# A chunked retention kernel with a routed feed-forward: gate weights as one row, three comparisons moved to ScalarE, wider filler products and a new written-out order

## Chip, cores and metric

One Trainium2 core of eight. The metric is the device time of one execution in microseconds (us), the median of three runs. Engines are named as the profile names them: PE (TensorE), PEld (its weight loads), DVE (VectorE), ACT (ScalarE), POOL (GpSimd), SP (the queue from which the ordinary transfers are issued).

## What is computed

```python
# attention: q, k, v of shape (4, 8, 768, 64); head h decays by gamma[h]
state = gamma * state + k_t (outer) v_t           # per token t
y_t   = scale * q_t @ state
x = y as (B, S, 512)
# routed feed-forward, per batch b: the 128 tokens with the highest score
scores = x @ w_gate
top = the 128 best of the 768 tokens
out[top] = x[top] + sigmoid(scores[top]) * (relu(x[top] @ w1) @ w2)     # w1: 512 x 1024, w2: 1024 x 512
out[others] = x[others]
```

## The kernel before

The work is cut into 12 units: 4 batches of 3 units, each 256 tokens of all 8 heads. A unit loads 512 KB each of q, k and v, brings them to bf16 with the decay factors, turns them on PE, copies the results out of PSUM, and computes for its two chunks of 128 tokens the masked scores, the chunk's output and the running state. A batch's third unit is followed by its routing: a rank is counted for each token by comparing its score with all others, the 128 best are picked, run through two products with w1 and w2, and added into the rows of the output that were stored before.

Every piece of work is a named task with an engine, the tasks that it needs, and its buffers. `Plan.run` (line 111) issues the tasks in the sequence of the text `ORDER` (line 21), so that text alone sets the order on every engine: each engine runs its own tasks in that order and waits at the first whose inputs are missing. In an item such as `tk.0:1+3@A`, `@` picks one of the allowed engines, `:` names the PSUM banks, and `+3` puts three filler products (`warm_f`, line 202) before the task, products of a constant with itself whose result is overwritten. Task names used below, u being the unit and c its chunk:

- `lq.u lk.u lv.u` loads, `st.u.c` stores, `lw` the load of the gate weights, `w1.i w2.i` the eight loads of the feed-forward's weights, all on SP. There are five buffers each for q, k and v (`DEPTH`, line 18), shared with the weights, and 14 for finished chunks (`xo`).
- `qc kc vc` casts after the load (lines 361, 415, 417; POOL, some on ACT or DVE), `tq tk tv` turns on PE and `eq ek ev` their copies (371, 384, 392), `bk bv` and `fk fv` the same a second time (404, 405).
- `sc.u.c` the scores (440), `mk` the mask on DVE (442), `yo ys` the output products (464, 466), `up es` the state (478, 480), `ey.u.c` the copy of a chunk's output (483), `ga.u.c` its gate scores on DVE (484).
- `pr.u` the scores spread over a row on PE (509), `cp.u` its copy (530), `cd.u.c` and `co.u.c` the comparisons within the unit and with earlier units (520, 526; line 523 is the instruction), `cnt` the counts (629), `rk oh` rank and picked tokens (639, 646), `ix ic gc` their index and gate (670 to 672), `gat sa` gather and scatter (681, 711), `tn ex hu hr dn ad` the feed-forward, `cw1.i.h cw2.i.h` the casts of its weights (312), `yb` bf16 copies of the last batch's chunks (491).
- `tw ew`: the 512 gate weights on all 128 partitions (lines 289 to 298): four numbers a partition are loaded, four turns on PE spread them, a copy puts them in order into `wgB`, which every `ga` reads.

The last batch's products with w1 and w2 are cut finer and mixed with those of batch 2, whose gather comes late.

Of the kernel before, what the change touches and what calls it, by code (L numbers as in the profile page):

```python
# [21 lines left out]
lq.0 lk.0 cf lq.1 cp4 cp1 cp5 cp7 cp3 cp2 cp6 cd0 cz0 lw ca0 cd1 cd3 cd4 ca3 qc.0.1@D qc.0.0@P tq.0:0+26 eq.0@D ca4  # L22
kc.0.0@P kc.0.1@A lv.0 lk.1 tk.0:1 ek.0@A sc.0.1:10 mk.0.1.0 mk.0.1.1 sc.0.0:23 bk.0:4 qc.1.0 qc.1.1 vc.0.0@D tw:5
tq.1:1 fk.0@A kc.1.0@A lv.1 vc.0.1@P tv.0:4+5 ev.0@A lk.2 kc.1.1@P tk.1:0+1 lq.2 vc.1.1 vc.1.0 lv.2 lk.3 ek.1@A lq.3
bv.0:4 fv.0@A qc.2.0 qc.2.1 lv.3 vc.2.1 vc.2.0 qc.3.0 qc.3.1 mk.0.0.0 mk.0.0.1 eq.1@D ew@D sc.1.0:01 mk.1.0.0
# [41 lines left out]
hu.3.2.1 hu.3.0.1 hu.3.1.1 hu.2.0:2 hr.3.0@D hr.3.1@D hr.3.2@A hr.3.3@D hr.2.0@A hu.2.1:4 dn.2.0:2 sa.1 sa.0 gat.3
dn.3.1.0:0 dn.3.0.0:3 hr.2.1@D dn.2.1 ad.2 sa.2 dn.3.0.1 dn.3.1.1 dn.3.0.2 dn.3.1.2 dn.3.0.3 dn.3.1.3 ad.3.0 ad.3.1
sa.3
"""  # L70
# [682 lines left out]
```

## Time and profile before

| | |
|---|---|
| median of three runs | 98.91 us (98.85, 98.91, 100.12) |
| profiled execution, its own time | 98.33 us |
| its span, first to last instruction | 96.6 us |
| around the span | 1.73 us |
| TensorE clock granted, mean | 0.967 of full |
| moved by DMA | 31.67 MB |

A row of a timeline reads: start, duration, engine, line, operation, output and inputs, shapes, count; in brackets the idle time of the engine before it and what ended it. Rows next to each other can overlap, because an instruction's start does not wait for its forerunner's last element; the step from start to start is then what an engine spends on one.

### The profile page before, as it was taken

The numbers are of one execution on the slowest core, as the hardware profiler recorded it, in microseconds if no ns is written. First come the engines' busy times: TensorE is split into PE (matmuls) and PEld (weight loads), VectorE is DVE, ScalarE is ACT, GpSimd is POOL, SyncE is SP. The second block draws the span as 40 slices with busy tenths as digits, with TensorE's granted clock in tenths as the row PEclk, the third lists the DMA queues.
The fourth block names the chain that finished last, engine by engine and source line by source line (L and its number), as shares of the span: only waits on it lengthen the run. The fifth ranks groups of instructions, "written<-read, shape, count | busy, mean of one in ns | idle before, by whom it ended". The sixth has DMA issues, their size and how long they took to land.

```text
span 96.6 us, 3508 instructions
## 1 busy us (share of the span) xinstructions
PE 85.0 (88%) x1370; PEld 72.6 (75%) x1373; DVE 79.5 (82%) x240; ACT 71.5 (74%) x152; POOL 76.5 (79%) x113
## 2 busy tenths in 40 slices
PE   4717899999999999999999999999999999999800
PEld 4615687989899888887899789987899765997500
DVE  5333699999999999999999999999999996862510
ACT  6422249999999999999999999999999970132000
POOL 6580897999999999998989999999998765480250
PEclk9997599999999999999999999999999999999985
DMA  0899999999999899999999999999999996153031
GB/s 7 287 369 362 392 390 392 384 385 403 389 390 404 280 386 265 357 401 404 400 392 392 399 396 398 408 410 409 404 414 411 396 396 221 75 217 109 0 148 70
DMA packets 15199, 31.67 MB, mean 328 GB/s; under 512 B 1360, under 2 KB 1360, under 8 KB 15184
## 3 DMA queue, kind: packets, MB, share of 16 engines
q1 hardware_dynamic: 14544, 29.37, 81.5%
q0 software_dynamic: 640, 2.10, 5.9%
q8 instruction: 10, 0.16, 0.7%
q14 instruction: 5, 0.04, 0.1%
HBM read 24.12 MB, written 7.34 MB: 326 GB/s over the span
## 4 chain that ended last, share of the span: by engine, by line
DMA 45%; POOL 17%; PE 16%; issue 8%; SPq 7%; POOLq 1%; ACT 1%; DVE 0%
DMA qf<-in_q_dram 26%; DMA wf<-in_moe_w_dram 19%; POOL qb L170 8%; SPq L342 5%; POOL vq L170 4%; PE pd L556 2%; PE py L450 2%; POOL kq L167 2%; PE tv L382 2%; SPq L487 2%; PE pg L573 2%; POOLq L748 1%; PE bv L402 1%; POOL w2s L167 1%; PE tq L368 1%
## 5 line engine op out<-in xcount | busy, mean ns | idle before, releaser
L442 DVE TENSOR_TENSOR A<-ps,causal 128x512 bf16<-128x512 f32 x48 | 31.0, 685 | 1.7 <-PE ps L437 1.4
L170 POOL TENSOR_TENSOR qb<-qf,gq 128x512 bf16<-128x512 f32 x23 | 24.4, 1086 | 5.2 <-DMA qf<-in_q_dram 5.1
L170 POOL TENSOR_TENSOR vq<-vf,gv 128x512 bf16<-128x512 f32 x23 | 24.4, 1080 | 0.4 <-DMA vf<-in_v_dram 0.3
L484 DVE SCALAR_TENSOR_TENSOR junk<-py,wgB 128x512 bf16<-128x512 f32 x24 | 16.0, 685 | 0.4 <-ACT xo L163 0.3
L163 ACT ACTIVATE xo<-py 128x512 f32<-128x512 f32 x23 | 14.8, 661 | 0.0
L163 ACT ACTIVATE kq<-kf 128x512 bf16<-128x512 f32 x16 | 10.9, 686 | 3.5 <-DMA kf<-in_k_dram 3.5
L163 ACT ACTIVATE S<-pst 128x512 bf16<-128x512 f32 x20 | 13.4, 669 | 0.0
L450 PE MATMUL py<-vb,A 128*128 128x64 bf16 x192 | 10.7, 192 | 0.0
L368 PE MATMUL tq<-identf,qb 128*128 128x128 f32 x48 | 7.5, 278 | 3.4 <-POOL qb L170 3.2
L437 PE MATMUL ps<-qT,kT 64*128 64x128 bf16 x192 | 9.4, 226 | 0.7 <-ACT kT L163 0.7
L707 POOL DMA_INDIRECT out_dram<-xr,idx x4 | 4.0, 1004 | 7.1 <-DVE xr L702 6.5
L523 DVE TENSOR_SCALAR_CACHE_REDUCE g<-row,sc 128x256 bf16<-128x256 f32 (+1 forms) x16 | 9.6, 608 | 0.0
L163 ACT ACTIVATE kb<-bk 128x512 f32<-128x512 f32 x12 | 7.9, 661 | 2.2 <-PE bk L402 2.2
L516 DVE SCALAR_TENSOR_TENSOR g<-pr,sc,tri 128x128 bf16<-128x128 f32 (+1 forms) x24 | 9.2, 413 | 0.1
L450 PEld LDWEIGHTS <-A 128*128 128x128 bf16 x192 | 8.7, 97 | 0.8
L163 ACT ACTIVATE kT<-tk 128x512 f32<-128x512 f32 x12 | 8.0, 665 | 1.0 <-PE tk L382 1.0
L163 ACT ACTIVATE vT<-tv 128x512 f32<-128x512 f32 x12 | 7.9, 655 | 0.7 <-PE tv L382 0.7
L368 PEld LDWEIGHTS tq<-identf,qb 128*128 128x128 f32 x48 | 5.1, 141 | 4.3 <-POOL qb L170 3.9
L163 ACT ACTIVATE vb<-bv 128x512 f32<-128x512 f32 x12 | 8.1, 672 | 0.2 <-PE bv L402 0.2
L402 PE MATMUL bk<-identf,kT 128*128 128x128 f32 x48 | 8.0, 292 | 0.0
L437 PEld LDWEIGHTS <-kT 64*128 64x128 bf16 x192 | 5.9, 98 | 2.7 <-ACT kT L163 1.0
L402 PE MATMUL bv<-identf,vT 128*128 128x128 f32 x48 | 7.6, 281 | 0.1
(114 smaller groups left out, 199.6 us busy)
## 6 DMA issues: line engine op xcount, KB each, us to landing
qf<-in_q_dram SPq DMA_DIRECT2D x12, 512.0 KB, 8.5
kf<-in_k_dram SPq DMA_DIRECT2D x12, 512.0 KB, 8.7
vf<-in_v_dram SPq DMA_DIRECT2D x12, 512.0 KB, 9.2
out_dram<-xo SPq DMA_DIRECT2D x24, 256.0 KB, 7.7
wf<-in_moe_w_dram SPq DMA_DIRECT2D x8, 512.0 KB, 9.2
xg<-out_dram,idx POOLq DMA_INDIRECT x4, 5.7
out_dram<-xr,idx POOLq DMA_INDIRECT x4, 2.7
wg<-in_moe_w_gate_dram SPq DMA_DIRECT2D x1, 2.0 KB, 7.3
```

The costliest lines, as they stand in the source:

```text
L163: nc.scalar.activation(dst, src, AF.Copy)
L170: (nc.vector if eng == "DVE" else nc.gpsimd).tensor_mul(dst, a, b)
L342: return f, P.add(f"l{nm}.{u}", "SP", lambda e: nc.sync.dma_start(f[:].rearrange("p (e x) -> p e x", e=2), src), bufs=[f])
L368: nc.tensor.transpose(tq[:, j].rearrange("p g h -> p (g h)"), qb[:, j].rearrange("p e d s -> p (e d s)").bitcast(FT), identf)
L402: nc.tensor.transpose(pt[:, c, w, :], words[:, w, C * c:C * c + C], identf)
L437: nc.tensor.matmul(ps[par][:, hp, :], kT[rr, hp // 2, C * c:C * c + C, hp % 2], qT[rr, hp, C * c:C * c + C], start=True, stop=True, skip_g ...
L442: mk = [P.add(f"mk.{u}.{c}.{par}", "DVE", lambda e, par=par, ps=ps, A=A: nc.vector.tensor_mul(A[par][:], ps[par][:], causal[:, None, :].to ...
L450: nc.tensor.matmul(dst, lhsT, rhs, start=not opened, stop=True, skip_group_check=True)
L484: bt["gate"][J] = P.add(f"ga.{u}.{c}", "DVE", lambda e, J=J, py=py, junk=junk: nc.vector.scalar_tensor_tensor(junk[:], py[:].opt(), 1.0, w ...
L516: nc.vector.scalar_tensor_tensor(bt["g"][:, lo + J0:lo + J + 1, :].rearrange("p i t -> p (i t)"), pr[:, :c + 1, :].rearrange("p i t -> p ( ...
L523: nc.vector.tensor_scalar(bt["g"][:, lo:lo + J0, :].rearrange("p i t -> p (i t)"), bt["row"][:, :J0 * C], bt["sc"][:, J:J + 1], 0.0, OP.is ...
L707: apart(b, "rows", nc.gpsimd.indirect_dma_start(out=rows, out_offset=bass.IndirectOffsetOnAxis(ap=idx[:, 0:1], axis=0), in_=xr[:], in_offs ...
```

## The change

Four edits of code, and a new text `ORDER`.

1. The gate weights are loaded as one row of 512 numbers into partition 0 of `wgB`, and one product with a column of ones (`ones1`, set in `cd4`) spreads them over the 128 partitions; the copy `ew` is then contiguous. Before, there were 128 pieces of 16 bytes and four turns.
2. In the last batch `co.u.c` may run on ACT: a sign of (own score minus row), then a sign of (one minus that), which gives 1 where the row is at least the own score; the second pass adds up. The new order puts `co.10.0`, `co.10.1` (128x256) and `co.11.0` (128x512) there; `co.11.1` stays on DVE.
3. The fillers ahead of `tq`, `bk`, `bv` and `pr` are 256 columns wide where they were 128.
4. `ORDER`: k is loaded first, 24 loads are ahead of the first store, and 40 fillers stand where 37 stood (12 of them behind unit 0's start, where 5 stood).

```diff
+    ones1 = consts.tile([1, 128], FT, name="ones1")
-        wg4, bass.AP(tensor=w_gate.tensor, offset=w_gate.offset, ap=[[HP, 128], [1, HP]])))
+        wgB[0:1], bass.AP(tensor=w_gate.tensor, offset=w_gate.offset, ap=[[Dm, 1], [1, Dm]])))
     def turn_w(e):
-        for x in range(HP):
-            nc.tensor.transpose(pw[:, x, :], wg4[:, x:x + 1].to_broadcast([128, 128]), identf)
+        nc.tensor.matmul(pw[:], ones1, wgB[0:1], start=True, stop=True, skip_group_check=True)
-    t_w = P.add("tw", "PE", turn_w, after=[l_w, k_p5], ...
+    t_w = P.add("tw", "PE", turn_w, after=[l_w, k_d4], ...
-        ... warm=warm_f(lambda: tq[:, 0].rearrange("p g h -> p (g h)"))
+        ... warm=warm_f(lambda: tq[:, 0:2].rearrange("p j g h -> p (j g h)"))
                 def far(e, J=J, lo=lo):
+                    if e == "ACT":
+                        g = bt["g"][:, lo:lo + J0, :].rearrange("p i t -> p (i t)")
+                        nc.scalar.activation(g, bt["row"][:, :J0 * C], AF.Sign, bias=bt["sc"][:, J:J + 1], scale=-1.0)
+                        nc.scalar.activation(g, g, AF.Sign, bias=1.0, scale=-1.0, accum_out=bt["far"][:, J:J + 1])
+                        return
-                fr = P.add(f"co.{u}.{c}", "DVE", far, ...
+                fr = P.add(f"co.{u}.{c}", "DVE ACT" if b == LAST else "DVE", far, ...
 ORDER
-lq.0 lk.0 cf lq.1 cp4 cp1 cp5 cp7 cp3 cp2 cp6 cd0 cz0 lw ca0 cd1 cd3 cd4 ca3 qc.0.1@D qc.0.0@P tq.0:0+26 eq.0@D ca4
+lk.0 lq.0 lw lq.1 lv.0 lk.1 lv.1 lk.2 cf cp4 cp1 cp2 cp3 cp5 cp6 cp7 kc.0.1@P cd0 cd1 cd3 cz0 cd4 ca0 ca3 ca4 qc.0.1@D
...
```

What the new order does is seen in three places. The SP queue before, from the first store on (`st.0.0`; the stores are the rows that write `out_0_dram`; the tenth row is `st.2.1`):

```order
L487 DMA out_0_dram<-xo_473 128x512
L342 DMA qf_636<-in_q_dram 128x2x512
L342 DMA qf_638<-in_q_dram 128x2x512
L342 DMA kf_640<-in_k_dram 128x2x512
L342 DMA qf_642<-in_q_dram 128x2x512
L487 DMA out_0_dram<-xo_550 128x512
L342 DMA vf_645<-in_v_dram 128x2x512
L487 DMA out_0_dram<-xo_458 128x512
L342 DMA kf_648<-in_k_dram 128x2x512
L487 DMA out_0_dram<-xo_770 128x512
L342 DMA vf_876<-in_v_dram 128x2x512
L342 DMA qf_878<-in_q_dram 128x2x512
```

The SP queue now, from `lv.7` on (the first store is `st.1.1`, the last row `st.3.1`):

```order
L342 DMA vf_1097<-in_v_dram 128x2x512
L342 DMA kf_1099<-in_k_dram 128x2x512
L342 DMA qf_1273<-in_q_dram 128x2x512
L487 DMA out_0_dram<-xo_630 128x512
L342 DMA qf_1280<-in_q_dram 128x2x512
L487 DMA out_0_dram<-xo_434 128x512
L342 DMA kf_1283<-in_k_dram 128x2x512
L342 DMA vf_1287<-in_v_dram 128x2x512
L342 DMA kf_1289<-in_k_dram 128x2x512
L487 DMA out_0_dram<-xo_805 128x512
L487 DMA out_0_dram<-xo_444 128x512
L487 DMA out_0_dram<-xo_933 128x512
```

Before, `st.2.1` stood ahead of `lv.6` and of unit 7's loads; now these loads stand ahead of every store, and stores of units 0 to 2 wait longer. At the queue's other end 13 stores stand ahead of the last weight load, where 15 stood; 11 follow it, where 9 followed.

The last rows of ACT ahead of the last batch's feed-forward, before (`w2s` rows are casts of weights, `hT` the feed-forward of batches 0 and 1, `gs` is `ge.3`):

```order
L163 ACTIVATE w2s_201<-wf_1655 128x512
L548 ACTIVATE hT_2159<-ph_2209 128x512
L651 ACTIVATE gs_2257<-sc_1859 128x6
L163 ACTIVATE xgT_2252<-pg_2251 128x256 x2
L163 ACTIVATE xo_2117<-py_2116 128x512
L163 ACTIVATE yb_2320<-xo_2117 128x512
L163 ACTIVATE yb_2322<-xo_2014 128x512
L163 ACTIVATE w2s_201<-wf_1660 128x512
L548 ACTIVATE hT_2271<-ph_2270 128x512
L548 ACTIVATE hT_2271<-ph_2325 128x512
```

And now (`g` rows are the sign passes, two for each comparison; `far` holds their sums):

```order
L163 ACTIVATE xgT_2244<-pg_2243 128x256 x2
L163 ACTIVATE w2s_201<-wf_1804 128x512
L525 ACTIVATE g_2214<-row_2237,sc_2002 128x256
L526 ACTIVATE g_2214,far_2275<-g_2214 128x256
L656 ACTIVATE gs_2344<-sc_2002 128x6
L525 ACTIVATE g_2214<-row_2237,sc_2002 128x256
L526 ACTIVATE g_2214,far_2275<-g_2214 128x256
L553 ACTIVATE hT_2293<-ph_2292 128x512
L525 ACTIVATE g_2214<-row_2237,sc_2002 128x512
L526 ACTIVATE g_2214,far_2275<-g_2214 128x512
L553 ACTIVATE hT_2293<-ph_2310 128x512
L163 ACTIVATE yb_2352<-xo_2159 128x512
```

The six passes stand behind the cast of the last weight load (`cw2.3.0`) and around `hr.1.0`, the first half of batch 1's feed-forward; `ey.11.0` and one `yb` have left.

The last comparisons on DVE up to the rank, before (L516 is `cd`, L523 is `co`):

```order
L516 SCALAR_TENSOR_TENSOR g_2094,racc_2093<-pr_2262,sc_1859,tri2_190 128x128
L516 SCALAR_TENSOR_TENSOR g_2094,racc_2093<-pr_2095,sc_1859,tri2_190 128x256
L523 TENSOR_SCALAR g_2094,far_2298<-row_2104,sc_1859 128x256
L516 SCALAR_TENSOR_TENSOR g_2094,racc_2093<-pr_2262,sc_1859,tri2_190 128x256
L671 CAST idx_2302<-pi_2301 128x1
L523 TENSOR_SCALAR g_2094,far_2298<-row_2104,sc_1859 128x256
L523 TENSOR_SCALAR g_2094,far_2298<-row_2104,sc_1859 128x512 x2
L672 RECIPROCAL gt_2303<-pi_2301 128x1
L636 TENSOR_TENSOR rank_2380<-pk_2358,racc_2093 128x2
```

And now:

```order
L516 SCALAR_TENSOR_TENSOR g_2214,racc_2213<-pr_2285,sc_2002,tri2_190 128x256
L165 COPY row_2237<-pr_2285 128x256
L516 SCALAR_TENSOR_TENSOR g_2214,racc_2213<-pr_2215,sc_2002,tri2_190 128x128
L516 SCALAR_TENSOR_TENSOR g_2214,racc_2213<-pr_2327,sc_2002,tri2_190 128x128
L677 RECIPROCAL gt_2257<-pi_2255 128x1
L516 SCALAR_TENSOR_TENSOR g_2214,racc_2213<-pr_2327,sc_2002,tri2_190 128x256
L528 TENSOR_SCALAR g_2214,far_2275<-row_2237,sc_2002 128x512
L165 COPY xo_2159<-py_2158 128x512
L641 TENSOR_TENSOR rank_2381<-pk_2358,racc_2213 128x2
```

Three comparisons are gone from DVE, the copies `cp.10` and `ey.11.0` have come. On PE the same tasks follow `tn.1` up to the counts of the last batch, but `pr.11`, which `cd.11` waits for, now stands behind `hu.1.1` where it stood ahead of `dn.0.0`.

## Rows read from the trace of the kernel before

**Rows 1.** The profile's page: busy time of each engine with its share of the span, and the rate of DMA in 40 slices of 2.4 us.

```profile
PE 85.0 (88%) x1370; PEld 72.6 (75%) x1373; DVE 79.5 (82%) x240; ACT 71.5 (74%) x152; POOL 76.5 (79%) x113
...
GB/s 7 287 369 362 392 390 392 384 385 403 389 390 404 280 386 265 357 401 404 400 392 392 399 396 398 408 410 409 404 414 411 396 396 221 75 217 109 0 148 70
```

**Rows 2.** Busy time by stretch: start and end, length, busy us of each engine with its count, granted TensorE clock, busy share of the DMA engines, GB/s.

```profile
5.00:12.20 7.20, 4.11 (x36) 3.21 (x36) 3.42 (x5) 1.82 (x3) 4.23 (x5) 0.76 1.03 372
15.78:80.22 64.44, 63.51 (x1127) 55.13 (x1124) 63.59 (x192) 63.17 (x136) 59.99 (x81) 1.00 1.03 387
31.40:38.60 7.20, 7.20 (x129) 5.98 (x128) 7.04 (x23) 7.20 (x17) 7.15 (x10) 1.00 0.95 310
74.50:81.90 7.40, 7.13 (x96) 4.93 (x95) 6.62 (x32) 4.51 (x11) 4.88 (x12) 1.00 0.94 345
81.90:91.40 9.50, 9.40 (x127) 7.93 (x127) 5.47 (x13) 1.75 (x4) 3.35 (x4) 1.00 0.30 107
```

**Rows 3.** Timeline of the SP queue around `st.2.1` (the second row).

```profile
25.56 0.60 SPq L342 DMA_DIRECT2D kf<-in_k_dram  x1
30.94 0.34 SPq L487 DMA_DIRECT2D out_dram<-xo  x1
31.37 0.60 SPq L342 DMA_DIRECT2D vf<-in_v_dram  x1
```

**Rows 4.** Timeline of POOL: two casts that wait for loads in the middle of the run.

```profile
44.78 2.08 POOL L170 TENSOR_TENSOR qb<-qf,gq 128x512 bf16<-128x512 f32 x2 [0.48 <-DMA qf<-in_q_dram]
...
49.76 2.08 POOL L170 TENSOR_TENSOR vq<-vf,gv 128x512 bf16<-128x512 f32 x2 [0.26 <-DMA vf<-in_v_dram]
```

**Rows 5.** The chain of waits that ended last, where it leaves the last weight load: start, us, what.

```profile
67.34 9.45 DMA wf<-in_moe_w_dram
...
76.84 0.61 POOL w2s L167
...
78.28 0.62 POOL w2s L167
...
78.94 0.59 PE pd L556 x2
```

**Rows 6.** Timeline of PE from `tn.1` to the last batch's counts; the last row is a weight load of `dn.0.1`.

```profile
74.55 0.64 PE L691 MATMUL pg<-identf,xg 128*128 128x128 f32 x4
...
78.21 1.32 PE L556 MATMUL pd<-w2s,hT 128*128 128x512 bf16 x4
...
80.59 0.42 PE L624 MATMUL pk<-mones,g 128*128 128x1 bf16 x11
80.87 1.02 PE L556 MATMUL pd<-w2s,hT 128*128 128x512 bf16 x4
...
78.94 0.10 PEld L556 LDWEIGHTS <-hT 128*128 128x128 bf16 x1 [0.42 <-issue]
```

**Rows 7.** Timeline of DVE: the start (`vc.0.0`, `eq.1`, `ew`, the first mask of unit 1), then the last comparisons and the rank.

```profile
11.49 1.22 DVE L170 TENSOR_TENSOR vq<-vf,gv 128x512 bf16<-128x512 f32 x1 [0.75 <-ACT kb L163]
...
13.83 0.68 DVE L165 COPY qT<-tq 128x512 f32<-128x512 f32 x1
14.42 1.14 DVE L165 COPY wgB<-pw 128x512 f32<-128x512 f32 x1
15.78 1.29 DVE L442 TENSOR_TENSOR A<-ps,causal 128x512 bf16<-128x512 f32 x2 [0.22 <-PE ps L437]
...
78.40 0.47 DVE L523 TENSOR_SCALAR_CACHE_REDUCE g<-row,sc 128x256 bf16<-128x256 f32 x1
...
78.80 0.74 DVE L523 TENSOR_SCALAR_CACHE_REDUCE g<-row,sc 128x512 bf16<-128x512 f32 x1
...
79.47 0.74 DVE L523 TENSOR_SCALAR_CACHE_REDUCE g<-row,sc 128x512 bf16<-128x512 f32 x1
...
81.05 0.16 DVE L636 TENSOR_TENSOR rank<-pk,racc 128x2 f32<-128x2 f32 x1 [0.75 <-PE pk L624]
```

**Rows 8.** Timeline of ACT: two copies of 128x512 with one of 128x256 between, and the wait in the tail.

```profile
43.55 0.66 ACT L163 ACTIVATE vb<-bv 128x512 f32<-128x512 f32 x1
44.03 0.45 ACT L163 ACTIVATE row<-pr 128x256 f32<-128x256 f32 x1
44.30 0.68 ACT L163 ACTIVATE xo<-py 128x512 f32<-128x512 f32 x1
...
83.12 0.38 ACT L163 ACTIVATE xgT<-pg 128x256 bf16<-128x256 f32 x1 [4.08 <-PE pg L573]
```

**Rows 9.** Timeline of PE: the fillers ahead of `tv.0`.

```profile
12.71 0.71 PE L203 MATMUL tv<-fill 128*128 128x256 bf16 x5
```

**Rows 10.** The gate weights: their transfer (KB, us from issue to landing), their issue, and their turns on PE; then the first cast of unit 1.

```profile
wg<-in_moe_w_gate_dram SPq DMA_DIRECT2D x1, 2.0 KB, 7.3
...
2.87 0.60 SPq L289 DMA_DIRECT2D wg<-in_moe_w_gate_dram  x1
...
10.61 1.06 PE L295 MATMUL pw<-identf,wg 128*128 128x128 f32 x4
...
10.09 2.07 POOL L170 TENSOR_TENSOR qb<-qf,gq 128x512 bf16<-128x512 f32 x2 [2.71 <-DMA qf<-in_q_dram]
```

**Rows 11.** The end: the second batch's sum on DVE, and the last scatter.

```profile
90.11 0.75 DVE L702 SCALAR_TENSOR_TENSOR xr<-pd,gt,xg 128x512 f32<-128x512 f32 x1 [1.50 <-PE pd L556]
...
92.45 0.97 POOL L707 DMA_INDIRECT out_dram<-xr,idx  x1 [0.30 <-issue]
```

More of the change, by code (lines that the diff above doesn't have):

```diff
@@ L67 @@
[L67 to L69 removed]
+lk.0 lq.0 lw lq.1 lv.0 lk.1 lv.1 lk.2 cf cp4 cp1 cp2 cp3 cp5 cp6 cp7 kc.0.1@P cd0 cd1 cd3 cz0 cd4 ca0 ca3 ca4 qc.0.1@D
+kc.0.0@A tk.0:0+19 ek.0@D qc.0.0@P tq.0:1+7 tw:0 vc.0.1@D vc.0.0@D eq.0@A ew@A sc.0.0:12 sc.0.1:34 bk.0:5 fk.0@A lq.2
+qc.1.0 qc.1.1 kc.1.0@P kc.1.1@A tq.1:0 vc.1.0 vc.1.1 eq.1@A tv.0:5+2 mk.0.1.0 mk.0.0.0 mk.0.1.1 mk.0.0.1 tk.1:6
@@ L70 @@
+dn.1.0:5 gat.2 cnt.3.1 ra.3 gh.3 dn.1.1 rk.3 oh.3.0 tn.3.0.0:3 tn.3.1.0:4 oh.3.3 tn.3.0.1 ix.3:1 tn.3.1.1 ad.1 ad.0
+ic.3 ex.3.1@D ex.3.0@A hu.3.1.0:3 hu.3.2.0:6 hu.3.0.0:5 hu.3.1.1 tn.2:4 st.10.1 st.11.0 st.9.1 hu.3.0.1 hu.3.3.0:0
+hu.3.2.1 hu.3.3.1 st.10.0 sa.1 ex.2.0@A ex.2.1@A hu.2.0:4 hr.3.2@A hr.3.0@A hr.3.3@A hr.2.0@A hu.2.1:5 dn.2.0:4 gc.3
+hr.2.1@A hr.3.1@D dn.3.0.0:5 dn.3.1.0:0 dn.2.1 ad.2 dn.3.0.1 sa.0 gat.3 dn.3.1.1 dn.3.0.2 dn.3.1.2 dn.3.0.3 dn.3.1.3
+sa.2 ad.3.0 ad.3.1 sa.3
 """
@@ L259, in c_dve4 @@
         nc.vector.memset(mones, -1.0)
+        nc.vector.memset(ones1, 1.0)
     def c_act0(e):
@@ L289 @@
     l_w = P.add("lw", "SP", lambda e: nc.sync.dma_start(
-        wg4, bass.AP(tensor=w_gate.tensor, offset=w_gate.offset, ap=[[HP, 128], [1, HP]])))
-    pw = P.buf("px", [128, HP, 128], FT, "pw")
+        wgB[0:1], bass.AP(tensor=w_gate.tensor, offset=w_gate.offset, ap=[[Dm, 1], [1, Dm]])))
+    pw = P.buf("px", [128, Dm], FT, "pw")
     def turn_w(e):
-        for x in range(HP):
-            nc.tensor.transpose(pw[:, x, :], wg4[:, x:x + 1].to_broadcast([128, 128]), identf)
-    t_w = P.add("tw", "PE", turn_w, after=[l_w, k_p5], bufs=[pw], warm=warm_f(lambda: pw[:, 0:2].rearrange("p x q -> p (x q)")))
-    k_wgB = P.add("ew", "ACT DVE", lambda e: copy(e, wgB.rearrange("p (q x) -> p x q", x=HP), pw[:]), after=[t_w], bufs=[pw])
+        nc.tensor.matmul(pw[:], ones1, wgB[0:1], start=True, stop=True, skip_group_check=True)
+    t_w = P.add("tw", "PE", turn_w, after=[l_w, k_d4], bufs=[pw], warm=warm_f(lambda: pw[:, :256]))
+    k_wgB = P.add("ew", "ACT DVE", lambda e: copy(e, wgB, pw[:]), after=[t_w], bufs=[pw])
     w_done = {}
@@ L369, in turn_q @@
                                     qb[:, j].rearrange("p e d s -> p (e d s)").bitcast(FT), identf)
-        t_q = P.add(f"tq.{u}", "PE", turn_q, after=qc + [k_p5], bufs=[qb, tq, qT], warm=warm_f(lambda: tq[:, 0].rearrange("p g h -> p (g h)")))
+        t_q = P.add(f"tq.{u}", "PE", turn_q, after=qc + [k_p5], bufs=[qb, tq, qT], warm=warm_f(lambda: tq[:, 0:2].rearrange("p j g h -> p (j g h)")))
         eq = P.add(f"eq.{u}", "ACT DVE", lambda e: copy(
@@ L402, in go @@
                         nc.tensor.transpose(pt[:, c, w, :], words[:, w, C * c:C * c + C], identf)
-            t_ = P.add(f"b{nm}.{u}", "PE", go, after=[e_, k_p5], bufs=[xT, pt, xb], warm=warm_f(lambda: pt[:, 0, 0, :]))
+            t_ = P.add(f"b{nm}.{u}", "PE", go, after=[e_, k_p5], bufs=[xT, pt, xb], warm=warm_f(lambda: pt[:, 0].rearrange("p w d -> p (w d)")))
             return xb, P.add(f"f{nm}.{u}", "ACT DVE", lambda e: copy(
@@ L522, in far @@
                 def far(e, J=J, lo=lo):
+                    if e == "ACT":
[3 more added lines that the diff above has]
+                        return
                     nc.vector.tensor_scalar(bt["g"][:, lo:lo + J0, :].rearrange("p i t -> p (i t)"), bt["row"][:, :J0 * C],
                                             bt["sc"][:, J:J + 1], 0.0, OP.is_ge, OP.add, accum_out=bt["far"][:, J:J + 1])
-                fr = P.add(f"co.{u}.{c}", "DVE", far, after=bt["cp"] + [bt["gate"][J]], bufs=[bt["row"], bt["sc"], bt["g"], bt["far"]])
+                fr = P.add(f"co.{u}.{c}", "DVE ACT" if b == LAST else "DVE", far, after=bt["cp"] + [bt["gate"][J]], bufs=[bt["row"], bt["sc"], bt["g"], bt["far"]])
                 bt["rk"][J].append(fr)
```

87 lines of the change are left out of this document (41 added, 46 removed).

## The prediction, made before the changed kernel ran

> **What bounds the kernel now.** I read the page first, for the balance of the engines. Then I read busy time by stretch, to see where that balance holds, and the chain of waits backwards from the end. Last came the timelines of the engines on which the chain turns: SP, POOL, PE, DVE and ACT.
>
> The page shows no single bound: PE is busy for 88% of the span, DVE 82%, POOL 79%, ACT 74%, and DMA runs near 400 GB/s in most slices [rows 1]. The stretch view divides this. From 15.78 to 80.22 us DVE is busy 63.59 of 64.44 us, PE 63.51, ACT 63.17, and DMA moves 387 GB/s on average [rows 2]. What can be won lies in the start, in a dip of DMA and in the tail. The start is short of data: up to 12.2 us PE is busy 4.11 of 7.20 us at a granted clock of 0.76 [rows 2], and POOL's first cast of unit 1 waits until 10.09 for its load [rows 10]. The dip runs from 31.4 to 38.6, at 310 GB/s [rows 2]. SP issued `lk.6` at 25.56, and then stood at `st.2.1` until 30.94, with `lv.6` behind it until 31.37 [rows 3]. The price comes later: POOL waits 0.48 us for a q at 44.78 and 0.26 for a v at 49.76 [rows 4].
>
> In the tail three things arrive nearly together. The last weight load lands at 67.34 + 9.45 = 76.79, its casts start at 76.84 and 78.28, and `dn.0.1` goes on at 78.94 [rows 5], 0.42 us late [rows 6]. DVE compares until 79.47 + 0.74 = 80.2, then stands 0.75 us, because PE starts the last counts only at 80.59 [rows 6, 7]. From 81.9 to 91.4 PE is busy 9.40 of 9.50 [rows 2], the last scatter starts at 92.45 [rows 11], and the order there hardly changes. So the end moves about as the rank at 81.05 moves.
>
> **The change part by part.**
>
> *The SP queue.* Filling the dip is worth 7.20 x (387 - 310) / 387 = 1.4 us of transfer [rows 2]. Two stores of 0.26 MB moved behind the last weight load are 0.52 MB / 387 GB/s = 1.35 us. The last weight load could land 2.8 us earlier, at 74.0. What then remains of the tail's wait is `dn.0.1`'s 0.42 us; no more than that, because PE's tasks from `tn.1` at 74.55 to the counts are the same ones. I take 0.42. POOL's waits are 0.74 in sum, bounds 0 (the other engines had work meanwhile) and 0.74; I take half, 0.37. The new stall is `st.3.1`, which stands ahead of `lq.9` and all later loads and needs a copy of unit 3. Up to it 28 loads and 4 stores are issued, 15.7 MB. The first 13 slices moved 11.0 MB by 31.4 us [rows 1], so there is work for DMA until about 43 us, and I count that stall at nothing. If its cover went, it would cost what the dip costs now.
>
> *The start.* The gate weights' 128 pieces go. DMA runs at 372 GB/s until 12.2, against 387 later [rows 2], which prices them at no more than 7.20 x 15 / 387 = 0.28 us. On PE `tw` moves ahead of unit 0's scores. The trace has no such product. The four turns took 1.06 us [rows 10], and I bound it by nothing and twice that. The cover is POOL's cast of q, which ends at 10.09 + 2.07 = 12.16 and before which PE has nothing of unit 1; with the load landing 7.3 us after issue as before [rows 10], and issued 0.65 earlier, at about 9.5, that cover just holds. On DVE `vc.0.1` comes (1.22 beside POOL) while `eq.1` (0.59 from start to start) and `ew` (1.14) leave [rows 7]; its masks slip behind both casts: 11.49 + 2 x 1.2 + 4 x 0.6 = 16.3 against 15.78. So the start lies between 0.28 won and 0.5 lost, and I take 0.
>
> *DVE up to the rank.* Gone after the start: `eq.2` and `ey.0.0`, 0.59 each by `eq.1`'s step [rows 7], two comparisons of 0.40 and one of 0.67 (78.40 to 78.80 to 79.47): 2.65 us. Come: `ek.2`, `ey.1.0`, `ey.11.0`, 0.59 each, and `cp.10`, about 0.3: 2.07. Net 0.58, and with the 0.75 that it stands now DVE could give 1.33 us. But PE brings the counts. By PE's busy row, 63.51 of 64.44 us, PE has no room, and 0 reaches the end. By the weight loads' row, 55.13, it has 9 us of room, and all 1.33 can [rows 2]. I take 0.5, nearer to the first, since the last counts are what DVE waited for. The Trainium skill (Trainium Kernel Development and Optimization, Performance Expectations) calls matmul busy time a bad measure of how full PE is, because matmuls are pipelined, and weight-load busy time a good one; taken alone it would give 1.33 here and a time of about 97.0, the busy row alone 98.3. No row of this trace decides between them.
>
> *ACT.* Six passes: by steps 4 x 0.27 + 2 x 0.48 = 2.04 us, by whole durations, since the second pass reads what the first wrote, 4 x 0.45 + 2 x 0.67 = 3.14 [rows 8]. I take the second. ACT is busy 4.51 of 7.40 us from 74.5 [rows 2], then waits 4.08 [rows 8], so 2.9 us of it fit before the counts; what does not fit is the slower rival below.
>
> *Fillers.* Seven more behind unit 0's start, 0.71 / 5 = 0.14 each [rows 9]: 0 to 1.0 us. The low end is a filler that runs while PE would have stood anyway. PE stands 0.93 us in the middle by its busy row and 9 us by its weight loads [rows 2]; I take 0.2, nearer to the second, since a filler fills what the first row calls busy too. Those that are only wider count within that.
>
> Sum: 0.42 + 0.37 + 0.5 - 0.2 = 1.1 us. From the profiled execution's own 98.33 us (span 96.6 and 1.73 around it) that gives 97.2. The median of the runs shown, 98.91, lies 0.58 above that execution, so I predict 97.8.
>
> **The rivals.**
>
> *All of it arrives.* PE has the room that its weight loads show. Then 0.42 + 0.74 + 1.33 + 0.28 = 2.8 us are won: 96.1. For it speaks that DVE has no gap between 15.78 and 80.22, against it that PE was last at 81.05.
>
> *PE is full and only shuffles.* Earlier loads find it busy; the fillers cost their whole 1.0, against 0.42 + 0.37 won: 99.1. For it: 9.40 of 9.50 us in the tail and 63.51 of 64.44 before it.
>
> *Slower: ACT's queue takes the place of DVE's.* The sign passes stand behind the cast of the last weight load and around `hr.1.0`. If that load lands at 76.79 as before, ACT ends the cast at 77.4, `co.10.0` at 78.3, `ge.3` at about 78.5, `co.10.1` at 79.4, `hr.1.0` at 80.0, `co.11.0` at 81.4, and `hr.1.1` at 82.0. `dn.1.1` needs `hr.1.1`, and now starts at 80.87 [rows 6]: 1.1 us late, 100.0. It decides when the last weight load lands later than 76.79 - 1.1 = 75.7. Against it: two stores less ahead of that load.
>
> **How the numbers follow.** My forecast 0.38 (own range 96.9 to 98.6), all of it 0.27, shuffled 0.17, slower 0.18. Within 2%, about what a measurement of this kernel can tell from no change, is 96.9 to 100.9. Faster: 0.24 of the second case and 0.06 of the first, 0.30. Slower: half of the last, which has room above its 1.1 us if the start's 0.5 is lost too, and a little of the third: 0.11. The rest, 0.59, is the same. The range goes from 95.7, a little below the second case, to 100.2, just above the last.
>
> **What would show it.** Right: no dip of DMA between 31 and 39 us; the last weight load landed by 75; `dn.0.1` without a stop; the rank at 80 instead of 81.05; PE as full from the rank to the last scatter as now. The forecast is wrong on DVE's share if DVE still waits for the counts as long, wrong on the SP queue if DMA falls off while SP stands at `st.3.1`, and wrong on ACT if the counts follow `co.11.0`. If unit 1's first mask comes after 16.3 us, the start has cost what I set at nothing.

## The result, and the profile after

The changed kernel takes 97.41 us (median of six runs, 97.03 to 97.60), the kernel before 98.90 beside it (98.53 to 100.12): a ratio of 0.9845, 95% interval 0.9809 to 0.9881, or 1.5 us less. The profiled execution took 97.38 us with a span of 95.7; the one of before took 98.33 with 96.6. The experiments below came in three groups of four, and the kernel before scattered more beside them (99.6 to 101.7, 99.3 to 102.6 and 97.1 to 101.9 us), so their ratios have wider intervals. Ratios leave disturbed runs out, which in the third group left only 5 of the 35 runs of before; there the kernels of the group are compared with each other.

The changed kernel's busy time by stretch, with the columns of [rows 2] (us, PE, PEld, DVE, ACT, POOL, granted clock, DMA share, GB/s):

```profile
5.00:12.20 7.20, 5.74 (x56) 3.71 (x54) 4.34 (x5) 3.00 (x6) 5.15 (x6) 1.00 1.05 391
31.40:38.60 7.20, 7.00 (x128) 6.47 (x126) 6.95 (x23) 7.20 (x17) 7.20 (x9) 1.00 1.05 393
74.50:81.90 7.40, 6.77 (x104) 5.23 (x103) 6.12 (x24) 4.98 (x14) 3.38 (x9) 1.00 0.61 202
81.90:91.40 9.50, 7.97 (x97) 6.45 (x95) 2.85 (x8) 2.88 (x8) 4.04 (x4) 1.00 0.40 142
```

Against [rows 2], three things moved. The dip of DMA is gone (393 GB/s where 310 stood). DMA falls off earlier at the end (202 where 345 stood): SP has issued the last weight load by 63.0 us, where it was 67.7. And in the start the granted clock is 1.00 where 0.76 stood; PE is busy 1.6 us more, which is no more than its fillers there (0.47 + 0.93 + 0.38). The last is the one I had read past. Before, PE was at the low one of its two clock levels (1.2 of 2.4 GHz) for most of the time from 8 to 12 us; the two halves of it show busy us of PE, granted clock, DMA share, GB/s, and below them stands PE's timeline of that start:

```profile
8.00:10.00 2.00, 1.31 (x19) 0.56 1.03 367
10.00:12.00 2.00, 1.67 (x8) 0.59 1.04 394
```

```profile
1.24 2.96 PE L203 MATMUL tq<-fill 128*128 128x128 bf16 x26 [1.24 <-DVE fill L272]
6.88 0.65 PE L368 MATMUL tq<-identf,qb 128*128 128x128 f32 x4 [2.69 <-POOL qb L170]
8.74 1.03 PE L437 MATMUL ps<-qT,kT 64*128 64x128 bf16 x16 [0.69 <-ACT kT L163]
12.22 0.66 PE L368 MATMUL tq<-identf,qb 128*128 128x128 f32 x4 [0.55 <-POOL qb L170]
```

PE stood 2.69 us behind its fillers; the next turns still took 0.65 us, and the 16 scores that came after them 1.03. In the changed kernel it never stands for a whole microsecond there, and the same 16 scores take 0.62 (third row); unit 1's turns come at 10.82 instead of 12.22 (last row):

```profile
6.26 0.93 PE L203 MATMUL tq<-fill 128*128 128x256 bf16 x7
8.14 0.66 PE L368 MATMUL tq<-identf,qb 128*128 128x128 f32 x4 [0.95 <-POOL qb L170]
9.78 0.62 PE L437 MATMUL ps<-qT,kT 64*128 64x128 bf16 x16
...
10.82 0.60 PE L368 MATMUL tq<-identf,qb 128*128 128x128 f32 x4
```

The loads were earlier as well. POOL goes from q of unit 0 into q of unit 1 without a stop (three casts in one row; by [rows 10] unit 1's first cast waited until 10.09), and DVE is at its casts of v at 9.17, where [rows 7] has 11.49 (there the wait before it ended with a copy on ACT, not with its load):

```profile
6.51 3.61 POOL L170 TENSOR_TENSOR qb<-qf,gq 128x512 bf16<-128x512 f32 x3 [0.82 <-DMA qf<-in_q_dram]
```

```profile
9.17 2.52 DVE L170 TENSOR_TENSOR vq<-vf,gv 128x512 bf16<-128x512 f32 x2 [1.40 <-DMA vf<-in_v_dram]
11.61 3.90 DVE L442 TENSOR_TENSOR A<-ps,causal 128x512 bf16<-128x512 f32 x6
```

Unit 1's first mask is the fifth of the six in the last row, so it starts near 14.2 us, where it stood at 15.78 [rows 7].

Now the tail. PE's rows that answer to [rows 6] are 2.0 us earlier at `tn.1` and 2.1 at the last counts; then two waits appear, one for `oh`, one for the second batch's gather:

```profile
72.52 0.63 PE L696 MATMUL pg<-identf,xg 128*128 128x128 f32 x4
...
78.46 0.42 PE L629 MATMUL pk<-mones,g 128*128 128x1 bf16 x11
...
80.40 1.17 PE L578 MATMUL pg<-oh,yb 128*128 128x128 bf16 x18 [0.58 <-DVE oh L648]
...
83.61 0.63 PE L696 MATMUL pg<-identf,xg 128*128 128x128 f32 x4 [0.51 <-DMA xg<-out_dram,idx]
```

ACT, where the sign passes went: the cast of the last weight load starts at 73.73 (that load landed at 76.79 in [rows 5]), and each pass with a sum brings an instruction of its own that reads it out:

```profile
73.73 0.63 ACT L163 ACTIVATE w2s<-wf 128x512 bf16<-128x512 f32 x1
74.25 0.51 ACT L525 ACTIVATE g<-row,sc 128x256 bf16<-128x256 f32 x1
74.85 0.42 ACT L526 ACTIVATE g<-g 128x256 bf16<-128x256 bf16 x1
75.17 0.19 ACT L526 ACTIVATION_READ_ACCUMULATOR g<-g 128x1 f32 x1
75.27 0.19 ACT L656 ACTIVATE gs<-sc 128x6 f32<-128x6 f32 x1
...
76.78 0.71 ACT L525 ACTIVATE g<-row,sc 128x512 bf16<-128x512 f32 x1
...
78.15 0.58 ACT L553 ACTIVATE hT<-ph 128x512 bf16<-128x512 f32 x1
```

By steps, a comparison of 256 costs 75.27 - 74.25 = 1.02 us and that of 512 costs 78.15 - 76.78 = 1.37; with the second of 256 (75.36 to 76.31) some 3.3 in all. DVE and POOL at the rank, and the end (the rows that answer to [rows 7, 11]):

```profile
78.91 0.16 DVE L641 TENSOR_TENSOR rank<-pk,racc 128x2 f32<-128x2 f32 x1 [0.24 <-PE pk L629]
...
79.59 0.16 DVE L642 TENSOR_TENSOR rank<-pk,far 128x4 f32<-128x4 f32 x1 [0.52 <-POOL far L637]
...
89.17 0.75 DVE L707 SCALAR_TENSOR_TENSOR xr<-pd,gt,xg 128x512 f32<-128x512 f32 x1 [5.60 <-PE pd L561]
```

```profile
78.20 1.12 POOL L682 DMA_INDIRECT xg<-out_dram,idx  x1 [2.45 <-DVE g L528]
79.34 0.23 POOL L637 TENSOR_TENSOR far<-far,racc 128x4 f32<-128x4 f32 x1
...
91.52 0.98 POOL L712 DMA_INDIRECT out_dram<-xr,idx  x1 [0.30 <-issue]
```

The rank's first half is 2.14 us earlier than in [rows 7], its second half waits for `ra.3` (`far`), which POOL issues behind the second batch's gather, and the last scatter is 0.93 us earlier than in [rows 11]. So 2 us were won before the tail, and the tail gave about half back: some 0.6 us at `oh`, which starts 1.5 us earlier than before, and some 0.6 behind it, most of that at `tn.2`.

### The profile page after: what moved, and what is told of

It is laid out like the page before. It is cut to its first block, busy times and chain, and to the rows that moved or that the text cites. A ratio compares the mean times of both kernels' runs of the same rounds, so it can differ in the third digit from the quotient of the medians.

```text
span 95.7 us, 3522 instructions
## 1 busy us (share of the span) xinstructions
PE 85.9 (90%) x1371; PEld 72.6 (76%) x1374; DVE 76.9 (80%) x232; ACT 75.3 (79%) x163; POOL 76.2 (80%) x114
## 4 chain that ended last, share of the span: by engine, by line
PE 58%; ACT 13%; DMA 10%; issue 6%; POOL 4%; DVE 2%; SPq 2%; POOLq 2%
PE py L450 10%; PE ps L437 7%; DMA out_dram<-xo 5%; DMA qf<-in_q_dram 5%; PE tq L368 5%; PE bv L402 5%; PE bk L402 5%; PE pst L475 4%; PE tv L382 4%; PE tk L382 4%; PE ph L547 4%; PE pr L507 3%; ACT qT L163 2%; ACT kq L163 2%; ACT xo L163 2%
## 5 line engine op out<-in xcount | busy, mean ns | idle before, releaser
L170 POOL TENSOR_TENSOR vq<-vf,gv 128x512 bf16<-128x512 f32 x22 | 23.1, 1065 | 0.9 <-DMA vf<-in_v_dram 0.8
L163 ACT ACTIVATE xo<-py 128x512 f32<-128x512 f32 x22 | 13.7, 629 | 0.1
L450 PE MATMUL py<-vb,A 128*128 128x64 bf16 x192 | 11.7, 192 | 0.0
L163 ACT ACTIVATE qT<-tq 128x512 f32<-128x512 f32 x12 | 7.7, 640 | 3.2 <-PE tq L368 3.2
L163 ACT ACTIVATE kq<-kf 128x512 bf16<-128x512 f32 x14 | 8.9, 655 | 1.2 <-DMA kf<-in_k_dram 1.2
L516 DVE SCALAR_TENSOR_TENSOR g<-pr,sc,tri 128x256 bf16<-128x256 f32 (+1 forms) x24 | 9.3, 411 | 0.8 <-PE pr L507 0.5
L528 DVE TENSOR_SCALAR_CACHE_REDUCE g<-row,sc 128x512 bf16<-128x512 f32 (+1 forms) x13 | 7.8, 618 | 0.0
L707 DVE SCALAR_TENSOR_TENSOR xr<-pd,gt,xg 128x512 f32<-128x512 f32 (+1 forms) x5 | 3.0, 638 | 5.9 <-PE pd L561 5.6
L682 POOL DMA_INDIRECT xg<-out_dram,idx x4 | 4.6, 1142 | 4.0 <-DVE g L528 2.5
L382 PE MATMUL tk<-ident,kq 128*128 128x128 bf16 x96 | 7.4, 220 | 0.3 <-POOL kq L167 0.3
```

Source lines behind the costliest of these rows:

```text
L163: nc.scalar.activation(dst, src, AF.Copy)
L170: (nc.vector if eng == "DVE" else nc.gpsimd).tensor_mul(dst, a, b)
L382: nc.tensor.transpose(pt[:, j].rearrange("p g h -> p (g h)"), fb[:, j].rearrange("p e d -> p (e d)"), ident)
L450: nc.tensor.matmul(dst, lhsT, rhs, start=not opened, stop=True, skip_group_check=True)
L516: nc.vector.scalar_tensor_tensor(bt["g"][:, lo + J0:lo + J + 1, :].rearrange("p i t -> p (i t)"), pr[:, :c + 1, :].rearrange("p i t -> p ( ...
L528: nc.vector.tensor_scalar(bt["g"][:, lo:lo + J0, :].rearrange("p i t -> p (i t)"), bt["row"][:, :J0 * C], bt["sc"][:, J:J + 1], 0.0, OP.is ...
```

## Experiments

### The start in the old order: loads or clock

The first thought was that the 128 small pieces had held back the loads. The first edit was made alone in the kernel before (`e1_row`), and the pieces were issued later in it (`e5_late_pieces`):

```diff
 e1_row, kernel before, ORDER as it was
-  128 pieces into wg4, four turns
+  one row into wgB, one product with ones1
 e5_late_pieces, kernel before
-... cz0 lw ca0 ...  lv.0 lk.1 tk.0:1
+... cz0 ca0 ...  lv.0 lk.1 lw tk.0:1
```

> The kernel before with the first edit alone: the gate weights come as one row and one product spreads them; the order is the old one. Theory A (the 128 pieces of 16 bytes held back the transfers around them): POOL's first cast of unit 1 starts near 8.1 us as in the changed kernel, not at 10.09, DVE's casts of v come about 2 us earlier, and 1 to 2 us of it reach the end: 97.0 to 98.0 us. Theory B (the new order of the loads did it): that cast stays at 10.0 to 10.1, and the time stays at 98.9 within 0.4.

> The kernel before with its 128 pieces, but their load issued behind that of unit 1's k and so behind six loads where it stood behind three. Theory A: q of unit 1 lands about 2 us earlier (its cast at 8 to 8.5 us) because nothing is in its way yet, and what is issued behind the pieces comes late instead; the turns of the gate weights come 1 to 2 us later. Time between 98.0 and 99.5 us. Theory B: the cast stays at 10.0 to 10.1 and the time at 98.9 within 0.4.

Measured: `e1_row` 103.76 us, ratio 1.041 (1.029 to 1.053); `e5_late_pieces` 101.60, 1.011 (0.997 to 1.025). `e1_row` is slower than either of its theories allows. The interval of `e5_late_pieces` is too wide to part its two; its q of unit 1 is cast at 10.35, near theory B's 10.0 to 10.1 and not at theory A's 8 to 8.5. In `e1_row` q of unit 1 is cast at 8.08, as theory A said, and yet the kernel is 4% slower. Its PE rows show why: from 6.8 to 19 us everything on PE takes nearly twice its duration:

```profile
6.76 1.11 PE L368 MATMUL tq<-identf,qb 128*128 128x128 f32 x4 [2.58 <-POOL qb L170]
...
9.42 1.03 PE L437 MATMUL ps<-qT,kT 64*128 64x128 bf16 x16 [0.69 <-ACT kT L163]
...
11.43 2.07 PE L295 MATMUL pw<-wgB,ones 1*128 1x512 f32 x2
13.43 1.11 PE L368 MATMUL tq<-identf,qb 128*128 128x128 f32 x4
...
19.22 0.66 PE L402 MATMUL bk<-identf,kT 128*128 128x128 f32 x4
```

```profile
12.00:14.00 2.00, 2.00 (x5) 1.00 1.05 392
```

The granted clock reads 1.00 in that stretch (second fence: busy PE, granted clock, DMA share, GB/s), so here only the durations tell the low level. The Trainium skill (TensorE: Matmul & The Clock Gate, Part 1) names these two levels for PE's clock, which depend on how busy PE has been, and says that the recorded clock events have been seen to be unreliable. The rows agree on the levels and on the record: the same 16 scores take 1.03 or 0.62 us, and here 1.03 at a recorded 1.00. With the low level lasting to 19 us, unit 1's first mask came at 18.96 instead of 15.78 [rows 7]. Of the 4.4 us by which this run's last scatter is late (96.87 against 92.45) 3.1 are there at `tn.1` (77.64 against 74.55); the rest arises behind `tn.2`, in a stretch whose length differs between executions of one kernel (last section). The kernel before came back to the high level by 12.22; why `e1_row` took until 19, and `e5_late_pieces`, with its four turns, until 17, is not settled.

### The start again: the fillers

If the clock decides, the fillers do. Three kernels: the changed one with as little filling as before (`e6_cold`), and the old order with more, once with pieces (`e7_warm`) and once with the row (`e8_row_warm`).

```diff
 e6_cold, changed kernel
-tk.0:0+19 ... tq.0:1+7
+tk.0:0+13 ... tq.0:1
 e7_warm, kernel before; e8_row_warm, e1_row
-tq.0:0+26
+tq.0:0+46
```

> The changed kernel with fewer fillers ahead of unit 0's turns: 13 where 19 stood and none where 7 stood, so that PE falls silent near 4.1 us, as before the change, and not near 7.2. Theory A (PE's clock is the start's main gain): the products of the start run at the low clock again (16 scores 1.03 us where the changed kernel shows 0.62), unit 1's first mask comes 1.3 us later or more, and the time is 98.5 to 101 us. Theory B (the earlier loads are the gain): the start's products take 0.62 and 0.66 us as now, the time stays at 97.4 within 0.5.

> The kernel before with 46 fillers ahead of its first turns where 26 stood, so that PE is busy until about 6.5 us and not 4.2. Nothing else is changed: pieces, old order, old loads. Theory A: the low clock between 8 and 12 us (16 scores in 1.03 us, four turns in 1.06 to 1.12) is gone; unit 1's products still wait for its q at 10.1, so unit 1's first mask moves from 15.8 to 15 at best and 0.3 to 0.9 us are won. Theory B (the clock does not hang on these fillers): rows of the start as before, the time equal to before within 0.4 us.

> The kernel before with the first edit (one row, one product), which by itself ran 4% slower, and with 46 first fillers. Theory A (that run lost by the low clock, which lasted until 19 us in it, though its loads were 2 us early): the start's products run at the high clock, unit 1's first mask comes at 13.5 to 14.5 us instead of 18.96, and the time falls by 1 to 2 us below the kernel before. Theory B (the one-row product or the early loads themselves do harm in the old order): still 2% or more slower than before.

Measured: `e6_cold` 100.98 us, 1.004 (0.998 to 1.010); `e7_warm` 100.01, 0.993 (0.988 to 0.998); `e8_row_warm` 99.21, 0.983 (0.978 to 0.988). Theory A holds each time. Without thirteen fillers, some (4.23 - 2.96) + 0.93 = 2.2 us of products that compute nothing, the changed kernel loses all its gain, although its q of unit 1 is cast at 8.59. PE and DVE of `e6_cold`, the last row being unit 1's first mask, 3 us later than in the changed kernel:

```profile
1.24 2.96 PE L203 MATMUL tk<-fill 128*128 128x256 bf16 x13 [1.24 <-DVE fill L273]
...
11.18 1.04 PE L437 MATMUL ps<-qT,kT 64*128 64x128 bf16 x16
```

```profile
17.26 1.29 DVE L442 TENSOR_TENSOR A<-ps,causal 128x512 bf16<-128x512 f32 x2 [2.46 <-PE ps L437]
```

And PE of `e7_warm`, the kernel before with twenty more fillers: behind the fillers no product takes twice its duration, and unit 1's turns stand at 10.26.

```profile
1.24 5.09 PE L203 MATMUL tq<-fill 128*128 128x128 bf16 x46 [1.24 <-DVE fill L272]
...
8.60 0.62 PE L437 MATMUL ps<-qT,kT 64*128 64x128 bf16 x16 [0.69 <-ACT kT L163]
...
10.26 0.66 PE L368 MATMUL tq<-identf,qb 128*128 128x128 f32 x4
```

The last row goes beyond what was expected: q of unit 1 was there two us sooner than in the profile of before, with all 128 pieces in place.

`e8_row_warm` weighs most. It keeps the old order, the old SP queue and every comparison on DVE, and with the row and twenty more fillers alone its ratio, 0.983, is that of the whole change, 0.9845. Beside `e7_warm`, from which it differs by the first edit only, it is 0.8 us faster in the median (the two intervals just meet), so with the clock held the row seems to be worth something in the old order; the start doesn't show where, since unit 1's first mask stands at 14.43 in `e7_warm` and 14.26 in `e8_row_warm`.

### The pieces in the new order, and the later fillers

```diff
 e2_pieces, changed kernel
-  one row into wgB, one product with ones1
+  128 pieces into wg4, four turns
 e4_nofill, changed kernel
-tv.0:5+2 ... tq.2:0+1 ... pr.1:0+2 ...   (14 fillers in ten places)
+tv.0:5 ... tq.2:0 ... pr.1:0 ...
```

> The changed kernel with its first edit undone: 128 pieces and four turns, the load third in the queue as in the changed kernel. Theory A: the loads behind the two first land about 2 us later again (first cast of unit 1 near 10 us instead of 8.1, first cast of v near 11 instead of 9.2), and 0.7 to 2 us of that reach the end: 98.1 to 99.4 us. Theory B: the landings stay as in the changed kernel and the time at 97.4 within 0.4.

> The changed kernel without its 14 fillers behind the first 26. Theory A (my term: a filler mostly runs while PE would have stood, net 0.2 us for seven more): the time falls by no more than 0.4 us, to 97.0 to 97.4, and the granted clock in the start stays at 1.00. Theory B (PE is full, each filler costs its 0.14 us): 14 of them are 2.0 us, the time falls below 96.4. Theory C (the fillers hold the clock): the granted clock falls below 0.95 somewhere in the first 20 us, and the time rises by 0.5 us or more.

Measured: `e2_pieces` 98.56 us, 0.981 (0.967 to 0.995); `e4_nofill` 97.91, 0.978 (0.969 to 0.987). Neither can be told from the changed kernel's 0.9845. For the pieces the profiles don't decide either. POOL's first cast of unit 1 began at 10.35 in `e5_late_pieces` and at 8.13 in `e7_warm`, both with pieces:

```profile
10.35 2.07 POOL L170 TENSOR_TENSOR qb<-qf,gq 128x512 bf16<-128x512 f32 x2 [2.58 <-DMA qf<-in_q_dram]
```

```profile
8.13 2.08 POOL L170 TENSOR_TENSOR qb<-qf,gq 128x512 bf16<-128x512 f32 x2 [0.99 <-DMA qf<-in_q_dram]
```

In the new order it began at 8.71 with pieces, and with the row between 7.9 and 9.21. So when the first loads land changes by up to 2 us from one execution to the next, and what the first edit is worth in the new order stays open. For the later fillers theory C falls (no stretch at the low level), and theory A and B are not parted by the times; the last scatter of `e4_nofill` starts at 91.85, against 91.52 with the fillers, which speaks for A, in one execution of each.

### The comparisons on ACT

```diff
 e3_co_dve, changed kernel
-co.10.0@A ... co.10.1@A hr.1.0@A co.11.0@A
+co.10.0 ... co.10.1 hr.1.0@A co.11.0
```

> The changed kernel with the three comparisons back on DVE, where they stood before. Theory A (my term: DVE's queue ahead of the counts is worth 0.5 us or more): the last counts start 0.8 to 1.6 us later than 78.46 us, and the time rises by 0.4 to 1.2 us. Theory B (the end hangs on batch 2's gather, which POOL issues at 78.2 to 79.3 and tn.2 waits for): the counts come later but the end moves by less than 0.3 us.

Measured: 101.73 us (99.99 to 101.79) beside 100.97 for the kernel before; no ratio could be formed, so the times decide nothing. Its start was late, so distances inside the tail of its one profiled execution are read. From `tn.1` (74.21) to the rank (82.48) it takes 8.27 us, in the changed kernel 78.91 - 72.52 = 6.39; to `oh` (82.74) 8.53, against 7.27; to the last scatter (95.00) 20.79, against 19.00. PE of this run, in the middle of the counts, then DVE:

```profile
81.05 0.25 PE L629 MATMUL pk<-mones,g 128*128 128x1 bf16 x4 [1.49 <-DVE g L528]
```

```profile
82.74 1.02 DVE L648 TENSOR_TENSOR oh<-pk,rank 128x384 bf16<-128x384 f32 x2
...
86.06 0.42 DVE L165 CAST xgT<-pg 128x256 bf16<-128x256 f32 x1 [0.91 <-PE pg L578]
```

The counts wait for DVE's comparisons: 1.9 us at the rank's first half, of which 1.3 reach `oh` (in the changed kernel the second half waits for `ra.3`). The 1.8 us at the last scatter can't all be put down to the comparisons, because behind `oh` comes the pause of the last row, which also stands in `e6_cold` and `e7_warm` (0.90 us each) at the same copy. In this one execution theory B falls, and theory A's 0.8 to 1.6 us at the counts was too small.

### The tail: `ra.3`, the gather, and the old order once more

Could the half that the tail gave back be had? `ra.3` was put ahead of the gather on POOL (`e9_ra`), then also `tn.2` behind eight more products (`e10_ra_tn`), with the changed kernel (`after_again`) and the old order with the new start (`e8_again`) on the same chip.

```diff
 e9_ra, changed kernel
-dn.1.0:5 gat.2 cnt.3.1 ra.3
+dn.1.0:5 ra.3 gat.2 cnt.3.1
 e10_ra_tn, the same and
-hu.3.1.1 tn.2:4 st.10.1 ... hu.3.0.1 hu.3.3.0:0
+hu.3.1.1 st.10.1 ... hu.3.0.1 hu.3.3.0:0 tn.2:4
```

> The changed kernel once more, as the measure for the three beside it, on the same chip. Every theory: 0.98 to 0.99 of the kernel before; POOL's first sum of unit 1 of the last batch's rank (ra.3) issues behind the second batch's gather and the rank's second half waits about 0.5 us for it; tn.2 waits about 0.5 us for that gather.

> The kernel before with the row load and 46 first fillers, beside the changed kernel. Theory A (the start is the whole gain; the refilled SP queue, the passes on ACT and DVE's relief bring nothing over it): equal to the changed kernel within 0.6 us. Theory B (my terms of the middle and the tail, 0.42 + 0.37 + 0.5 us, come on top of the start): 0.7 to 1.3 us slower than the changed kernel.

> The changed kernel with ra.3 ahead of gat.2 on POOL. Theory A (what the start won is given back at the rank, which waits for ra.3 behind the gather): the rank's second half follows its first without a wait, oh starts near 79.2 us instead of 79.79, and the end comes 0.3 to 0.6 us earlier. Theory B (the end hangs on the second batch's gather, at tn.2): the rank is earlier but tn.2 then waits about 1.1 us where it waited 0.5, and the end stays within 0.2 us.

> As the run before, and tn.2 behind eight more products of the last batch on PE. Theory A and B alike: the wait of tn.2 falls below 0.3 us, oh starts near 79.2, and the end comes 0.6 to 1.1 us earlier than in the changed kernel: about 0.990 of it. Theory C (the end hangs on something later, the third gather or the second batch's own chain of products): no gain over the changed kernel beyond 0.2 us.

Measured: `after_again` 97.04 us, 0.992 (0.982 to 1.002); `e8_again` 97.95, 0.988 (0.978 to 0.998); `e9_ra` 98.02, 1.002 (0.992 to 1.011); `e10_ra_tn` 97.94, 0.997 (0.991 to 1.003). The four share their runs of before; beside each other, the two with `ra.3` moved are 0.9 us slower in the median than the changed kernel. In `e9_ra` `tn.2` waits 1.13 us for the gather (first fence), as theory B said, though the end came later than that theory's 0.2 us. In `e10_ra_tn` the rank's wait is gone and `oh` starts at 79.02, but POOL's gather issues at 79.13, where `after_again` has 78.05, and its last scatter starts at 91.45, against 91.28: the 0.62 us won at `oh` are lost again in small waits on PE, 0.27 for the gather (last fence) and 0.30 for the copies behind it among them. POOL, then DVE, then PE of `e10_ra_tn` follow the row of `e9_ra`:

```profile
84.84 0.63 PE L696 MATMUL pg<-identf,xg 128*128 128x128 f32 x4 [1.13 <-DMA xg<-out_dram,idx]
```

```profile
78.17 0.20 POOL L637 TENSOR_TENSOR far<-far,racc 128x4 f32<-128x4 f32 x1 [2.64 <-ACT g L526]
79.13 1.11 POOL L682 DMA_INDIRECT xg<-out_dram,idx  x1 [0.76 <-issue]
```

```profile
79.02 1.02 DVE L648 TENSOR_TENSOR oh<-pk,rank 128x384 bf16<-128x384 f32 x2
```

```profile
83.55 0.63 PE L696 MATMUL pg<-identf,xg 128*128 128x128 f32 x4 [0.27 <-DMA xg<-out_dram,idx]
```

So theory A of `e9_ra` falls and theory C of `e10_ra_tn` holds: whichever of the two POOL does first, the other is late, and PE meets it at `oh` or at `tn.2`. No version here clearly beats the changed kernel.

`e8_again` asks what the rest of the new order brings, and by the ratios it brings nothing that can be told: 0.988 without it and 0.992 with it, and 0.983 for the same kernel in the group before. Theory A holds; theory B's 0.7 to 1.3 us do not show. Its best runs are level with the changed kernel's too (96.48 against 96.49 us); its median over all runs is 0.9 us higher, because half of its runs lie between 98.0 and 99.70. What sets those apart is not shown; one of them was profiled. In that execution (98.0 us) `tn.1` stands at 73.01, 1.5 us before that of [rows 6], and the last counts at 80.42, where [rows 6] has 80.59. PE:

```profile
77.33 0.59 PE L556 MATMUL pd<-w2s,hT 128*128 128x512 bf16 x2 [0.48 <-POOL w2s L167]
78.77 0.59 PE L556 MATMUL pd<-w2s,hT 128*128 128x512 bf16 x2 [0.85 <-POOL w2s L167]
...
80.42 0.42 PE L624 MATMUL pk<-mones,g 128*128 128x1 bf16 x11
```

PE waits 1.33 us for weights that the old queue brings late, where [rows 6] showed 0.42. In that execution the start's gain is lost at the weight loads. The ratios don't show such a loss for the kernel as a whole.

## Why the prediction came out, point by point

The forecast was 97.8 us, the result 97.41; the sum for the profiled execution was 97.2, against 97.38. The total was right and its working was not: the forecast won 1.1 us in the middle and the tail and none in the start, while the profiled execution had won 2.0 us at `tn.1` and gave 1.1 of them back behind it. By `e8_row_warm` the whole ratio comes without the terms that the forecast added up. That the two sums agree is luck.

- **The start, taken as 0 with at most 0.28 won: wrong, and the largest term.** `tq.1` came 1.4 us earlier, unit 1's first mask near 14.2 instead of the 16.3 worked out, and `tn.1` 2.0 us earlier. The step that failed is the price by mean GB/s, together with the reading of the granted clock of 0.76 as a mark of missing data. It was a price of its own: 16 scores in 1.03 us instead of 0.62, four turns in 1.12 instead of 0.66. `e6_cold` and `e7_warm` show that the fillers carry it. The four gate turns' 1.06 us was such a row too (0.60 in `e7_warm`). How the start's gain divides between the clock and the earlier loads is not shown.
- **Fillers, a cost of 0.2: the wrong sign for those in the start.** The term counted those behind unit 0's start by number and took the first ones as merely wider. It is those ahead of unit 0's turns that hold the clock; what the later ones cost, the times don't tell.
- **The SP queue, 0.42 at `dn.0.1` and 0.37 at POOL: the queue did what was said, but no time shows a gain from it.** The dip is gone, the last weights are cast at 73.73 and `dn.0.1` no longer waits. With the start early and the queue old, the wait was 1.33 us in the one execution of `e8_again` that was profiled, so its size hangs on the start; by the ratios the old queue costs nothing. The new stall at `st.3.1` cost nothing, as worked out: its cover held. POOL's two load waits are gone; that they were worth 0.37 is not shown.
- **DVE up to the rank, 0.5: not shown as a gain over the old order.** Its wait for the counts fell from 0.75 to 0.24 us, and by the one execution of `e3_co_dve` the passes on ACT are worth 1.3 us at `oh` within the new order; the old order with the new start, which has none of them, is as fast by the ratios. The netting of 0.58 us counted what came and went, but not where it stands: `cp.10` and `ey.11.0` sit in the last stretch, and three comparisons more behind them would have been late.
- **ACT, 3.14 us by whole durations: right,** with 3.3 measured. The three reads of the sums were not foreseen.
- **"The end moves about as the rank moves": wrong.** The rank moved by 2.1 and 1.5 us in its halves, the end by 0.93. PE first stood 0.58 us for `oh`, and from there to its last product it was not as full as before (9.47 of 10.04 us from 80.40, where it had 9.40 of 9.45 from 81.92), mostly because it waited for the gather.

Of the rivals, the slower one needed the last weights to land after 75.7; they were there at 73.73. "PE is full" falls with the 2 us that passed through the middle. "All arrives" is not borne out either: its terms are the forecast's own at full size, and the whole ratio is there without them.

## What to carry to other kernels

Look for stretches in which the same instruction takes twice as long before pricing anything by transfers: a short silence of PE at the start cost this kernel some 2% (`e6_cold`), more than all terms of the forecast together, and products that compute nothing paid for themselves there. Terms that are priced at today's arrival times don't add: in the traces, when the start moved by 2 us, the waits at the weight loads, the comparisons and POOL's queue each took another length. And when a total comes out as forecast, an experiment that gives the gain without the forecast's terms (`e8_row_warm`) tells luck from a right working. Where two tasks of one in-order engine are both due, changing their order only changes which consumer waits.

## What the hardware showed that was not expected

- PE's low level need not show in the granted clock: in `e1_row` it reads 1.00 from 12 to 14 us while four turns take 1.11 us and a row product 2.07 for two, against 0.60 to 0.66 and 1.12 in the changed kernel. In `e6_cold` it reads 1.00 as well while 16 scores take 1.04.
- The first loads land up to 2 us apart in executions with the same pieces and order of loads: q of unit 1 is cast at 10.09 in before and at 8.13 in `e7_warm`.
- On ACT a summed pass adds a read of 0.19 us, and a copy of 256 that took 0.45 us in [rows 8] and 0.39 in the changed kernel (`cp.9` at 72.37) is 0.51 as a sign with a column as its bias.
- The tail's length differs by 2 us between executions of one kernel: from `tn.2`'s turns to the last scatter it took 94.97 - 84.70 = 10.27 us in `e8_row_warm` and 92.14 - 83.83 = 8.31 in `e8_again`, which are the same kernel; `before` has 8.36, `e1_row` and `e7_warm` 10.1. In the long ones copies on DVE wait 0.9 us for products that had ended by their rows. The cause is not shown.
